# The low parts of the MLP's weights made by VectorE, and a table of places for every early step of an attention and ELU-MLP kernel

## The chip, the cores and the metric

The kernel runs on one core of one Trainium2 chip. The time is the device time of one execution, in microseconds (us). The median of three runs of the kernel before is 1268.88 us (1268.69 to 1268.94). The engines are TensorE (PE in the profile; PEld is its weight load), VectorE (DVE), ScalarE (ACT), GpSimd (POOL) and SyncE (SP), which here issues all transfers.

## The reference

```python
# q, k, v: (8, 12, 448, 64); w_in: (768, 2048); w_out: (2048, 768), all float32
q_n, k_n = rmsnorm(q, g_q), rmsnorm(k, g_k)
scores = q_n @ k_n.T / sqrt(64)
attn = exp(scores - max(scores)); attn = attn / (sum(attn) + 1e-9)
x = (attn @ v).transpose(0, 2, 1, 3).reshape(8 * 448, 768)
h = x @ w_in
g = where(h > 0, h, exp(min(h, 0)) - 1)
out = g @ w_out
```

## The kernel before

The program goes through 8 batches. A batch has 6 pairs of heads, and the 2 x 448 rows of a pair make 7 tiles of 128 rows: 42 tiles a batch, 336 in all, numbered T. For each tile TensorE writes scores of 128x448 to one of five PSUM banks (`s_mm`, L550), VectorE takes the negated maximum (`s_max`, L557), ScalarE the exponential with its sum (`s_exp`, L571), GpSimd adds 1e-9 to the sum and scales it (`s_z`, L575), and VectorE takes the reciprocal (`s_rec`, L583). In the first batch (`by_pe`) GpSimd then makes a diagonal matrix of the reciprocals (`s_diag`, L587), and TensorE multiplies with it, which normalises and transposes at once (`s_pe`, L595); the matmul is in float32. In later batches ScalarE and VectorE write the normalised tile as a float16 high part and low part (`s_hi` L611, `s_lo` L616), and a transfer transposes it (`s_tr`, L626). `attend` (L643) multiplies with v. Its output is the transpose of x, again as high and low part (L650, L657, L662).

The MLP takes every operand as a high and a low part in float16 and adds three products: high by high, high by low, low by high. For one batch it has 16 groups of 18 matmuls with w_in (L738) and 6 groups of 48 with w_out (L752), 576 in all. After each of the 16, `m1_out` makes the ELU in five steps: exp (ScalarE, L675), subtract 1 and cut at 0 (VectorE, L679), maximum with h (VectorE, L685), high part (ScalarE, L690), low part (VectorE, L693).

The weights are prepared once, beside the first batch's attention: w_in in 16 pieces of 128x768 (`conv_in`), w_out in 24 pieces of 128x512 (`conv_out`). Both begin with `conv`: a load, two steps of ScalarE on the bits (L238, L239), a shift (L244) and a join (L268) by VectorE which give the piece w, column sums by 13 or 9 small matmuls with a matrix of ones (L143), and a scale ws from their maximum (L146, L152). Then w_in's piece has: ScalarE makes ws times the identity (L289), GpSimd the high part (L292), TensorE for each half the float32 product of that diagonal with w less the high part (L299, L300), ScalarE copies the two halves out as the low part (L303). w_out's piece has three steps of GpSimd: the product with ws (L323), the high part from it (L328), the low part by subtraction (L334); the low part is stored to DRAM and loaded again for each batch. The column sums of w_out's first 7 pieces go to two banks of their own, those of the others to `av`, which also holds the output of `attend`.

Every engine does its instructions in the order in which the program issues them. That order is written out: time is counted in half-steps h, two for each tile. `SCHED` holds for every step of a piece, pair or batch the h at which it is issued; for tiles it is one row of offsets from 2T for the first batch and one for the rest. `rate` says how many of the MLP's matmuls have been issued by h, with an entry for every 7 half-steps. `run_tasks` issues what stands at h, `s_mm` one tile a step ahead, `attend` at fixed places.

Of the kernel before, what the change touches and what calls it, by code (L numbers as in the profile page):

```python
# [33 lines left out]
def tile_attention_then_elu_mlp(ctx: ExitStack, tc: tile.TileContext, qk, v, v_scan, gg, w_in, w_out, out):  # L34
# [184 lines left out]
    def conv(src, i, width, acol, bank, parts):  # L219
# [14 lines left out]
        def s_act():  # L234

            nc.scalar.activation(t, raw[:, :, 1].bitcast(F32), AF.Abs, scale=2.0**-112)  # L238
# [34 lines left out]
        steps = [load, s_act, s_shift, s_join, on_pe(s_sums), s_scale]  # L273
# [6 lines left out]
    def conv_in(f):  # L280
        hi, lo = (t[f].rearrange("p c n -> p (c n)") for t in (whi, wli))
        half = [slice(0, 384), slice(384, 768)]
        dgw = None
# [26 lines left out]

    def conv_out(i):
# [10 lines left out]
        def s_mult(w, ws):  # L322
            nc.gpsimd.tensor_scalar(  # L323
                out=w, in0=w, scalar1=ws, scalar2=2.0**UP, op0=ALU.mult, op1=ALU.mult
            )

        def s_high(w, ws):
            nc.gpsimd.tensor_scalar(  # L328
                out=hi, in0=view(w), scalar1=1.0, scalar2=0.0, op0=ALU.mult, op1=ALU.add
            )  # L330

        def s_low(w, ws):

            nc.gpsimd.tensor_tensor(out=low(w), in0=view(w), in1=hi, op=ALU.subtract)  # L334

        def s_store(w, ws):
# [3 lines left out]
            w_out, i, WO_W, most[:, i : i + 1], mb[i % 2] if i < WO_OWN else av,  # L340
            [s_mult, s_high, s_low, s_store],
# [133 lines left out]
    def v_steps(b):  # L475
# [16 lines left out]
        def four():  # L492
# [4 lines left out]
            ibits(vs, p2, -1, ALU.mult, (254 + 7 + UP) * E, ALU.add)  # L497
# [3 lines left out]
    def m_steps(b):  # L501
# [3 lines left out]
        sc, u, am, ui = (  # L505
            small(n, NF if n == "sc" else 1, bufs=3 if n == "u" else 2)
            for n in ("sc", "u", "am", "ui")
        )
        mscale[b] = sc, ui, u
# [7 lines left out]
        def powers():  # L517
            if b == 0:
                ibits(a_in, a_in, POWER, ALU.bitwise_and, 0, ALU.bitwise_or)

        def most_of():
# [144 lines left out]
    def m1_out(b, f, ph):  # L666
# [11 lines left out]

# [5 lines left out]

# [12 lines left out]
        return [one, two, three, four, five]  # L697

    def m2_out(b, d, py):
        u = mscale[b][2]  # L700
        y = ua = None

        def one():
# [3 lines left out]
                out=ua, in0=u, scalar1=a_out[:, d : d + 1], scalar2=2.0**-14, op0=ALU.mult,  # L707
                op1=ALU.mult,
# [10 lines left out]
        return [one, two, three]  # L719

    def mlp(b):
# [7 lines left out]
        for f in range(NF):  # L729
# [3 lines left out]
            ph = t_mo()  # L733
            for c in range(NC_):
# [47 lines left out]
    for T in reversed(range(NCHUNK)):  # L782
        k = 2 if by_pe(T) else 1
        hs = [2 * T + h for h in SCHED["tile"][k]]
        j = T % NJ
        if k < 2:
# [52 lines left out]
    for h in range(H0, LAST):  # L839
        T, odd = divmod(h, 2)  # L840

# [3 lines left out]
        ok = lambda t: 0 <= t < NCHUNK  # L845
# [4 lines left out]
        p, r = divmod(h, HP)  # L850

        if ok(T + 1) and odd == (h >= START):
            mm.append(lambda: s_mm(T + 1))
        if r == 7 and 0 <= p - 1 < NP:
# [160 lines left out]
```

## Time and profile before

| | |
|---|---|
| median of the runs | 1268.88 us |
| span of the profiled execution | 1267.6 us |
| TensorE busy | 1211.2 us, 96% |
| VectorE busy | 862.6 us, 68% |
| ScalarE busy | 822.3 us, 65% |
| GpSimd busy | 545.1 us, 43% |

The page gives the span of the profiled execution, from its first to its last instruction, and no other time of it; the median lies 1.3 us above the span. Times within the trace are counted from the span's start. A busy time is the union of an engine's instructions, which overlap a little, so that the sum of durations can be larger. Lines named L are those of the kernel before.

### The profile page before, as it was taken

The page shows a single profiled execution, that of the slowest core. Times are in us where ns is not written, and L with a number is a line of the kernel's source. Part 1 is how long each engine was busy: PE and PEld are TensorE (multiplying, and loading weights), DVE is VectorE, ACT ScalarE, POOL GpSimd, SP SyncE. Part 2 cuts the span into 40 slices and gives each one's busy share as a digit, 9 for nine tenths or more (in the row PEclk, how much of TensorE's full clock was granted, in tenths as well). Part 3 has the DMA queues.
Part 4 walks back from the last instruction along what each step waited for, and adds up shares of the span by engine and source line. Part 5 has one row for each costly group of instructions (what it writes and reads, how often), then busy time and mean ns, then how long its engine had stood idle before and what let it go on. Part 6 is the DMA issues. An engine that isn't in the chain of part 4 may idle for free.

```text
span 1267.6 us, 21938 instructions
## 1 busy us (share of the span) xinstructions
PE 1211.2 (96%) x7276; PEld 745.2 (59%) x7276; DVE 862.6 (68%) x1975; ACT 822.3 (65%) x1737; POOL 545.1 (43%) x879
## 2 busy tenths in 40 slices
PE   4899798899999999999999999999999999999998
PEld 2556444467556665576556755666557755675576
DVE  7767899977787568855886678756875678642410
ACT  7999878855676567754775567756766567542310
POOL 4755886774444433433444344434344334320000
PEclk9999999999999999999999999999999999999999
DMA  8665489989677986689576986698777957762011
GB/s 278 211 169 167 137 204 207 212 176 233 160 164 150 215 181 156 139 193 219 140 165 160 234 162 142 148 218 193 150 150 184 225 138 160 135 158 72 1 48 63
DMA packets 413392, 209.61 MB, mean 165 GB/s; under 512 B 369504, under 2 KB 389600, under 8 KB 413280
## 3 DMA queue, kind: packets, MB, share of 16 engines
q1 hardware_dynamic: 413280, 208.22, 70.9%
q8 instruction: 57, 0.93, 0.3%
q14 instruction: 55, 0.45, 0.1%
HBM read 93.52 MB, written 14.16 MB: 85 GB/s over the span
## 4 chain that ended last, share of the span: by engine, by line
PE 79%; DMA 1%; DVE 1%; SPq 0%; issue 0%; ACT 0%; ACTq 0%
PE m L752 22%; PE m L738 20%; PE s L752 11%; PE s L738 10%; PE s L550 8%; PE av L643 7%; DMA ptall<-p 1%; DVE w32s L268 0%; DVE gall L693 0%; DVE p L616 0%; PE av L143 0%; DVE e L685 0%; DVE st L557 0%; SPq L626 0%; SPq L448 0%
## 5 line engine op out<-in xcount | busy, mean ns | idle before, releaser
L557 DVE TENSOR_REDUCE st<-s 128x1 f32<-128x448 f32 x336 | 208.0, 619 | 154.4 <-PE s L550 152.8
L575 POOL TENSOR_SCALAR st<-st 128x1 f32<-128x1 f32 x336 | 83.7, 249 | 492.4 <-ACT s L571 454.3
L752 PE MATMUL m<-gall,whos 128*128 128x448 f16 x1024 | 282.2, 353 | 0.0
L752 PEld LDWEIGHTS <-whos 128*128 128x128 f16 x1536 | 221.9, 145 | 75.3 <-issue 2.6
L738 PE MATMUL m<-x,whi 128*128 128x448 f16 x916 | 253.9, 354 | 1.0 <-DVE x L657 0.6
L571 ACT ACTIVATE s<-s,st 128x448 f32<-128x448 f32 x294 | 177.9, 605 | 94.0 <-DVE st L557 91.7
L611 ACT ACTIVATE p<-s,st 128x448 f16<-128x448 f32 x294 | 185.1, 630 | 74.0 <-DMA ptall<-p 50.7
L738 PEld LDWEIGHTS <-whi 128*128 128x128 f16 x1536 | 149.5, 98 | 138.8 <-issue 3.9
L616 DVE SCALAR_TENSOR_TENSOR p<-s,st,p 128x448 f16<-128x448 f32 x294 | 198.9, 676 | 30.8 <-ACT p L611 29.1
L550 PE MATMUL s<-qkt 128*128 128x448 f16 (+1 forms) x768 | 184.1, 357 | 13.7 <-ACT gall L605 4.8
L752 PE MATMUL m<-gall,wls 128*128 128x448 f16 x512 | 181.2, 354 | 0.0
L738 PE MATMUL m<-x,wli 128*128 128x448 f16 x458 | 162.2, 354 | 0.0
L752 PE MATMUL s<-gall,whos 128*128 128x448 f16 x512 | 141.6, 353 | 1.3 <-DVE e L685 0.9
L752 PEld LDWEIGHTS <-wls 128*128 128x128 f16 x768 | 110.7, 144 | 41.4 <-issue 7.0
L738 PE MATMUL s<-x,whi 128*128 128x448 f16 x460 | 126.7, 353 | 0.2 <-DVE e L685 0.2
L738 PEld LDWEIGHTS <-wli 128*128 128x128 f16 x768 | 75.2, 98 | 75.6 <-issue 8.3
L690 ACT ACTIVATE gall<-e,ui 128x448 f16<-128x448 f32 x128 | 85.0, 664 | 38.9 <-DVE e L685 38.8
L550 PEld LDWEIGHTS <-qkt 128*128 128x128 f16 (+1 forms) x768 | 62.6, 100 | 78.5 <-issue 36.0
L693 DVE SCALAR_TENSOR_TENSOR gall<-e,ui,gall 128x448 f16<-128x448 f32 x128 | 90.1, 704 | 8.6 <-ACT gall L690 8.6
L643 PE MATMUL av<-ptall,vt 128*64 128x448 f16 x924 | 94.8, 353 | 0.7 <-DMA ptall<-p 0.7
L752 PE MATMUL s<-gall,wls 128*128 128x448 f16 x256 | 90.6, 354 | 0.0
L403 POOL TENSOR_TENSOR nat<-nat,r 128x896 f32<-128x896 f32 (+1 forms) x48 | 82.4, 1716 | 11.0 <-DVE r L393 8.0
(121 smaller groups left out, 1786.6 us busy)
## 6 DMA issues: line engine op xcount, KB each, us to landing
wls<-wl_d SPq DMA_DIRECT2D x48, 512.0 KB, 4.3
nat<-in_qk SPq DMA_DIRECT2D x48, 448.0 KB, 4.5
raws<-in_w_out SPq DMA_DIRECT2D x24, 512.0 KB, 4.4
qkt<-qkt SPq DMA_DIRECT2D x96, 112.0 KB, 4.0
out<-y SPq DMA_DIRECT2D x48, 224.0 KB, 2.7
vn<-in_v SPq DMA_DIRECT2D x38, 256.0 KB, 3.1
vscan<-in_v_scan SPq DMA_DIRECT2D x36, 224.0 KB, 3.7
whos<-in_w_in SPq DMA_DIRECT2D x10, 768.0 KB, 8.2
```

Of the source, the lines that this page charges most:

```text
L403: nc.gpsimd.tensor_tensor(out=n[:, a:], in0=n[:, a:], in1=r[:, a:], op=ALU.mult)
L550: nc.tensor.matmul(ps[r0 : r0 + n, :S], lhs, qq[:, 1, h * S : h * S + S], start=(t == 0), stop=(t == 2),)
L557: nc.vector.tensor_reduce(out=st[:, 0:1], in_=pss[T][:, :S], axis=AX.X, op=ALU.max, negate=True)
L571: nc.scalar.activation(e, ps, AF.Exp, bias=st[:, 0:1], accum_out=st[:, 1:2])
L575: nc.gpsimd.tensor_scalar(out=st[:, 1:2], in0=st[:, 1:2], scalar1=1e-9, scalar2=2.0 ** (UP - 7) if by_pe(T) else 2.0**-7, op0=ALU.add, op1 ...
L611: nc.scalar.activation(p16[:, :S], pss[T][:, :S], AF.Copy, scale=stats[T][:, 2:3])
L616: nc.vector.scalar_tensor_tensor(out=p16[:, S:], in0=ps[:, :S], scalar=r, in1=p16[:, :S], op0=ALU.mult, op1=ALU.subtract)
L643: nc.tensor.matmul(av[64 * h : 64 * h + 64, :S], vs[:, h], ps[h], start=(k == 0), stop=(k == len(terms) - 1),)
L690: nc.scalar.activation(g[:, 0], e, AF.Copy, scale=ui)
L693: nc.vector.scalar_tensor_tensor(out=g[:, 1], in0=e, scalar=ui, in1=g[:, 0], op0=ALU.mult, op1=ALU.subtract)
L738: nc.tensor.matmul(ph[:, :S], w[:, c, :], x[:, r, :], start=(c == 0 and i == 0), stop=last)
L752: nc.tensor.matmul(py[:, :S], w, g[:, r, :], start=(f == 0 and i == 0), stop=last)
```

## The change

The low part of a piece becomes one instruction of VectorE, `w * ws - high`, for both weights; the products on TensorE, their diagonal and the copies go. GpSimd makes w_out's high part directly as `w * ws`. The factor 2**13 of the former products now lies in the matrix of ones and in the later scales. In the first batch ScalarE makes `relu(1 - exp(h))` in place of VectorE's subtraction, and VectorE then takes the minimum with -h, so the sign of g turns and is turned back with the output's scale. The small step `s_z` is done by VectorE in the first batch. All column sums of w_out go to `av`. The table gets a row of its own for each of the first 96 tiles, for each MLP group of the first batch and for each of the first scores and `attend`, and `rate` an entry for each h. `EARLY`, by which parts of the first groups could be issued ahead, is 0.

```diff
-    nc.vector.memset(ones, 1.0)
+    nc.vector.memset(ones, 2.0**-UP)
...
-        steps = [load, s_act, s_shift, s_join, on_pe(s_sums), s_scale]
+        steps = [load, s_act, s_bits, s_shift, s_join, on_pe(s_sums), s_scale]
...
-        def s_diag(w, ws):
-            nonlocal dgw
-            dgw = pool.tile([128, 128], F32, tag="dgw", name="dgw", bufs=2)
-            nc.scalar.activation(dgw, ident, AF.Copy, scale=ws)
 
         def s_high(w, ws):
             nc.gpsimd.tensor_scalar(
-                out=hi, in0=w, scalar1=ws, scalar2=2.0**UP, op0=ALU.mult, op1=ALU.mult
+                out=hi, in0=w, scalar1=ws, scalar2=0.0, op0=ALU.mult, op1=ALU.add
             )
 
         def s_low(w, ws):
-            for i, c in enumerate(half):
-                pss[i] = mb[i]
-                nc.tensor.matmul(pss[i][:, :384], dgw, w[:, c], start=True, stop=False)
-                nc.tensor.matmul(pss[i][:, :384], neg, hi[:, c], start=False, stop=True)
-
-        def s_out(i):
-            nc.scalar.activation(lo[:, half[i]], pss[i][:, :384], AF.Copy)
+            nc.vector.scalar_tensor_tensor(
+                out=lo, in0=w, scalar=ws, in1=hi, op0=ALU.mult, op1=ALU.subtract
+            )
...
-        def s_mult(w, ws):
-            nc.gpsimd.tensor_scalar(
-                out=w, in0=w, scalar1=ws, scalar2=2.0**UP, op0=ALU.mult, op1=ALU.mult
-            )
-
         def s_high(w, ws):
             nc.gpsimd.tensor_scalar(
-                out=hi, in0=view(w), scalar1=1.0, scalar2=0.0, op0=ALU.mult, op1=ALU.add
+                out=hi, in0=view(w), scalar1=ws, scalar2=0.0, op0=ALU.mult, op1=ALU.add
             )
 
         def s_low(w, ws):
-
-            nc.gpsimd.tensor_tensor(out=low(w), in0=view(w), in1=hi, op=ALU.subtract)
+            nc.vector.scalar_tensor_tensor(
+                out=low(w), in0=view(w), scalar=ws, in1=hi, op0=ALU.mult, op1=ALU.subtract
+            )
...
-            w_out, i, WO_W, most[:, i : i + 1], mb[i % 2] if i < WO_OWN else av,
-            [s_mult, s_high, s_low, s_store],
+            w_out, i, WO_W, most[:, i : i + 1], av,
+            [s_high, s_low, s_store],
...
     def s_z(T):
         st = stats[T]
-        nc.gpsimd.tensor_scalar(
+        (nc.vector if by_pe(T) else nc.gpsimd).tensor_scalar(
...
         def two():
-
+            if b == 0:
+                nc.scalar.activation(e, e, AF.Relu, scale=-1.0, bias=one_c)
+                return
...
         def three():
-
+            if b == 0:
+                nc.vector.scalar_tensor_tensor(
+                    out=e, in0=ph[:, :S], scalar=mscale[b][3][:, f : f + 1], in1=e, op0=ALU.mult,
+                    op1=ALU.min,
+                )
+                return
...
-        k = 2 if by_pe(T) else 1
-        hs = [2 * T + h for h in SCHED["tile"][k]]
+        rows = SCHED["tile"]
+        hs = rows[T] if T < len(rows) - 1 else [2 * T + h for h in rows[-1]]
...
+    for T in range(NCHUNK):
+        n = SCHED["mm"][0]
+        pe_at.setdefault(n[T] if T < len(n) else 2 * T - 1, []).append((s_mm, T))
+    for p in range(NP):
+        n = SCHED["att"][0]
+        pe_at.setdefault(n[p] if p < len(n) else HP * p + HP + 7, []).append((attend, p))
...
     "tile": [
-        [-2.5, -1.5, -1.5, -0.5, 0.5, 1.5, 2.5, 5, 3],
+        [0.5, 1, 2, 2.5, 6, 6, 8],
...
-RATE_FROM = 85
+RATE_FROM = 25
```

What the table does to the order is shown at three places. In the rows, lines of before are those of the kernel before, and lines of after are a few lower.

TensorE, after the column sums of the second piece of w_in (bank `s3`). `dgw` is the diagonal, `m0` and `m1` the banks of the products, `qkt` the transposed q and k. Before, and then now:

```order
L143 MATMUL s3_70<-tiny_85,ones_80 128x64
L299 MATMUL m0_73<-w32s_140,dgw_238 128x384
L300 LDWEIGHTS neg_82
L300 MATMUL m0_73<-whi0_95,neg_82 128x384
L299 MATMUL m1_74<-w32s_140,dgw_238 128x384
L300 LDWEIGHTS neg_82
L300 MATMUL m1_74<-whi0_95,neg_82 128x384
L550 LDWEIGHTS qkt_208
L550 MATMUL s0_67<-qkt_208 128x448
```

```order
L542 MATMUL s1_68<-qkt_218 128x448
L542 LDWEIGHTS qkt_218
L542 MATMUL s0_67<-qkt_218 128x448
L542 LDWEIGHTS qkt_218
L542 MATMUL s0_67<-qkt_218 128x448
L542 LDWEIGHTS qkt_218
L542 MATMUL s2_69<-qkt_218 128x448
```

The products of the first piece stood between the sums and the scores of the first tile; now the scores of the first three tiles (banks `s1`, `s0`, `s2`) follow the sums at once, two matmuls each (the first of `s1` stands just ahead).

VectorE, around the maxima of the first tiles. L557 before and L549 now are `s_max`, L583 and L575 the reciprocal, L289 now is the low part of w_in's piece (`wli0`), L567 the small step `s_z`, L268 the join. Before, and then now:

```order
L268 SCALAR_TENSOR_TENSOR w32s_140<-whos_127,wts_139 128x768
L557 TENSOR_REDUCE st_287<-s0_67 128x1
L181 TENSOR_REDUCE mv_265<-gall_136 128x1
L146 TENSOR_REDUCE a_in_143<-av_72 128x1
L152 TENSOR_SCALAR ws_305<-a_in_143 128x1
L557 TENSOR_REDUCE st_308<-s1_68 128x1
L583 RECIPROCAL st_287<-st_287 128x1
L378 TENSOR_REDUCE ss_317<-qkt_300 128x14
```

```order
L289 SCALAR_TENSOR_TENSOR wli0_111<-w32s_140,ws_215,whi0_95 128x768
L549 TENSOR_REDUCE st_284<-s1_68 128x1
L549 TENSOR_REDUCE st_288<-s0_67 128x1
L268 SCALAR_TENSOR_TENSOR w32s_140<-whos_127,wts_139 128x768
L244 TENSOR_SCALAR wts_139<-wts_139 128x768
L549 TENSOR_REDUCE st_298<-s2_69 128x1
L144 TENSOR_REDUCE a_in_143<-av_72 128x1
L150 TENSOR_SCALAR ws_302<-a_in_143 128x1
L567 TENSOR_SCALAR st_284<-st_284 128x1
L567 TENSOR_SCALAR st_288<-st_288 128x1
L549 TENSOR_REDUCE st_312<-s3_70 128x1
L575 RECIPROCAL st_288<-st_288 128x1
```

The low part of the first piece stands ahead of the first two maxima, and the small steps of tiles stand behind the third maximum, together.

GpSimd, among the first pieces of w_out. L323, L328 and L334 before are product, high part and low part, L309 now is the high part; L587 and L579 are the diagonals of the tiles, L575 the small step. Before, and then now:

```order
L323 TENSOR_SCALAR w32s_140<-w32s_140,ws_1429 128x512
L575 TENSOR_SCALAR st_1420<-st_1420 128x1
L328 TENSOR_SCALAR whos_127<-w32s_140 128x512
L587 TENSOR_SCALAR dgz_1487<-ident_75,st_1420 128x128
L417 TENSOR_TENSOR nat_1109<-nat_1109,gst_141 128x448
L334 TENSOR_TENSOR w32s_140<-w32s_140,whos_127 128x512
L575 TENSOR_SCALAR st_1455<-st_1455 128x1
L323 TENSOR_SCALAR w32s_140<-w32s_140,ws_1484 128x512
L328 TENSOR_SCALAR whos_127<-w32s_140 128x512
L587 TENSOR_SCALAR dgz_1521<-ident_75,st_1455 128x128
```

```order
L579 TENSOR_SCALAR dgz_1385<-ident_75,st_1350 128x128
L410 TENSOR_TENSOR t16_1209<-nat_987,t16_1209 128x7x64
L309 TENSOR_SCALAR whos_127<-w32s_140,ws_1365 128x512
L579 TENSOR_SCALAR dgz_1473<-ident_75,st_1356 128x128
L309 TENSOR_SCALAR whos_127<-w32s_140,ws_1419 128x512
L579 TENSOR_SCALAR dgz_1497<-ident_75,st_1407 128x128
L309 TENSOR_SCALAR whos_127<-w32s_140,ws_1480 128x512
L579 TENSOR_SCALAR dgz_1524<-ident_75,st_1469 128x128
```

Between two diagonals GpSimd had up to three instructions of a piece and the small steps; now one instruction of a piece stands there.

## Rows read from the trace of the kernel before

**Rows 1.** The page: span, then busy time, share and count by engine.

```profile
span 1267.6 us, 21938 instructions
PE 1211.2 (96%) x7276; PEld 745.2 (59%) x7276; DVE 862.6 (68%) x1975; ACT 822.3 (65%) x1737; POOL 545.1 (43%) x879
```

**Rows 2.** Stretches: length; busy us (count) of PE, PEld, DVE, ACT, POOL; clock, DMA, GB/s.

```profile
0.00:24.00 24.00, 6.81 (x52) 4.24 (x53) 16.64 (x39) 17.22 (x23) 9.29 (x12) 1.00 0.83 272
24.00:148.00 124.00, 107.40 (x820) 71.00 (x818) 92.70 (x217) 119.57 (x240) 83.80 (x131) 0.99 0.62 185
148.00:314.00 166.00, 147.73 (x947) 88.27 (x947) 142.62 (x309) 122.50 (x242) 117.39 (x159) 0.98 0.90 199
314.00:1152.00 838.00, 837.29 (x4862) 510.57 (x4862) 582.32 (x1364) 537.94 (x1196) 333.33 (x573) 1.00 0.77 170
1152.00:1268.00 116.00, 111.95 (x602) 71.14 (x598) 28.29 (x49) 25.12 (x40) 1.32 (x5) 0.99 0.13 42
...
148.00:256.00 108.00, 91.81 (x601) 48.65 (x601) 101.41 (x215) 88.31 (x169) 81.69 (x105) 0.97 0.87 197
256.00:314.00 58.00, 55.92 (x346) 39.62 (x346) 41.21 (x95) 34.19 (x74) 35.70 (x55) 1.00 0.96 203
```

**Rows 3.** Timeline of VectorE at 313 us: start, length, line, operation.

```profile
313.19 0.61 DVE L557 TENSOR_REDUCE st<-s 128x1 f32<-128x448 f32 x1
```

**Rows 4.** PE's timeline at 44 us; lines: busy us, mean ns, idle before.

```profile
43.95 0.81 PE L299 MATMUL m<-w32s,dgw 128*128 128x384 f32 x2
...
45.56 0.54 PE L550 MATMUL s<-qkt 128*128 128x448 f16 x2
...
L303 ACT ACTIVATE wli<-m 128x384 f16<-128x384 f32 x32 | 15.4, 490 | 0.4 <-PE m L300 0.4
L289 ACT ACTIVATE dgw<-ident,ws 128x128 f32<-128x128 f32 x16 | 6.3, 396 | 0.0
L323 POOL TENSOR_SCALAR w32s<-w32s,ws 128x512 f32<-128x512 f32 x24 | 20.4, 849 | 7.6 <-DVE ws L152 3.7 <-DVE st L583 3.4
L334 POOL TENSOR_TENSOR w32s<-w32s,whos 128x512 f16<-128x512 f32 x24 | 29.6, 1238 | 1.1
L328 POOL TENSOR_SCALAR whos<-w32s 128x512 f16<-128x512 f32 x24 | 17.4, 727 | 1.4
L575 POOL TENSOR_SCALAR st<-st 128x1 f32<-128x1 f32 x336 | 83.7, 249 | 492.4 <-ACT s L571 454.3 <-ACT ex L571 26.6 <-DMA ptall<-p 6.0
...
L679 DVE TENSOR_SCALAR e<-e 128x448 f32<-128x448 f32 x16 | 8.2, 510 | 0.1
```

**Rows 5.** Single lines: duration ns min/median/max, or busy us and mean ns.

```profile
L268 DVE SCALAR_TENSOR_TENSOR w32s<-raws,wts x30: 671/946/1916, 14.6 to 272.0; 128x512 uint32<-128x512 uint32 x24, 128x768 uint32<-128x768 uint32 x6
L268 DVE SCALAR_TENSOR_TENSOR w32s<-whos,wts x10: 940/959/1820, 21.2 to 114.7; 128x768 uint32<-128x768 uint32 x10
...
L268 DVE SCALAR_TENSOR_TENSOR w32s<-raws,wts 128x512 uint32<-128x512 uint32 x18 | 17.7, 995 | 0.6 <-ACT raws L239 0.4
...
L693 DVE SCALAR_TENSOR_TENSOR gall<-e,ui,gall x128: 658/676/1481, 173.6 to 1212.1; 128x448 f16<-128x448 f32 x128
L685 DVE SCALAR_TENSOR_TENSOR e<-m,sc,e x85: 658/675/685, 169.3 to 1207.3; 128x448 f32<-128x448 f32 x85
...
L152 DVE TENSOR_SCALAR ws<-most 128x1 int32<-128x1 int32 x24 | 3.7, 154 | 0.8
...
L690 ACT ACTIVATE gall<-e,ui 128x448 f16<-128x448 f32 x128 | 85.0, 664 | 38.9 <-DVE e L685 38.8
```

**Rows 6.** Timelines of VectorE and GpSimd at 191 us.

```profile
191.66 1.34 DVE L679 TENSOR_SCALAR e<-e 128x448 f32<-128x448 f32 x1
...
191.43 1.32 POOL L334 TENSOR_TENSOR w32s<-w32s,whos 128x512 f16<-128x512 f32 x1
```

**Rows 7.** Lines of ScalarE, 148 to 314 us; PE's waits there: total, times, longest.

```profile
L611 ACT ACTIVATE p<-s,st 128x448 f16<-128x448 f32 x41 | 25.8, 630 | 21.0 <-DMA ptall<-p 12.2 <-DVE st L583 4.2 <-issue 3.4
...
PE av L143 <- DVE x L662: 3.7, 2, 2.4
```

More of the change, by code (lines that the diff above doesn't have):

```diff
@@ L70, in t_mo @@
         taken += 1
-        return mb[taken % 3]
+        return mb[(taken - 1) % 3]
     ident = const.tile([128, 128], F32, name="ident")
@@ L88, in tile_attention_then_elu_mlp @@
     nc.vector.memset(eps, 1e-6)
+    one_c = const.tile([128, 1], F32, name="one")
+    nc.vector.memset(one_c, 1.0)
     def cols(t, n):
@@ L254, in s_scale @@
             e = largest(bank, acol)
-            ws = small("ws")
+            ws = small("ws", bufs=4)
             ibits(ws, e, POWER, ALU.bitwise_xor, POWER, ALU.bitwise_and)
@@ L355, in load_v, with read_v @@
     def load_v(p):
-        if p in vn:
-            return
+        if p >= 2 * NPAIR - 1:
+            read_v(p)
+    def read_v(p):
         vn[p] = pool.tile([128, 4, 2, D], F32, tag="vn", name="vn", bufs=1)
@@ L496, in four @@
             vs = vscale[b] = small("vs")
-            ibits(vs, p2, -1, ALU.mult, (254 + 7 + UP) * E, ALU.add)
+            ibits(vs, p2, -1, ALU.mult, (254 + 7) * E, ALU.add)
         return [one, two, on_pe(three), four]
     def m_steps(b):
[L505 to L509, printed above, removed]
+        sc = u = am = ui = ns = None
         def mul(out, x, s1, s2=None):
@@ L517, in powers, with scales @@
         def powers():
+            nonlocal sc, u, am, ui, ns
+            sc, u, am, ui = (
+                small(n, NF if n == "sc" else 1, bufs=3 if n == "u" else 2)
+                for n in ("sc", "u", "am", "ui")
+            )
+            ns = small("ns", NF) if b == 0 else None
+            mscale[b] = sc, ui, u, ns
             if b == 0:
                 ibits(a_in, a_in, POWER, ALU.bitwise_and, 0, ALU.bitwise_or)
+        def scales():
+            mul(sc, a_in, vpow[b], 2.0 ** (-28 + UP))
+            if b == 0:
+                mul(ns, a_in, vpow[b], -(2.0 ** (-28 + UP)))
         def most_of():
@@ L695, in five @@
             )
-        return [one, two, three, four, five]
+        return SCHED["m1"][f if b == 0 else NF], [one, two, three, four, five]
     def m2_out(b, d, py):
-        u = mscale[b][2]
+        u, sign = mscale[b][2], -1.0 if b == 0 else 1.0
         y = ua = None
@@ L717, in three @@
             nc.sync.dma_start(out=out[d * 128 : (d + 1) * 128, b * S : (b + 1) * S], in_=y)
-        return [one, two, three]
+        return SCHED["m2"][d if b == 0 else NC_], [one, two, three]
     def mlp(b):
@@ L727, in wl_load @@
             nc.sync.dma_start(out=wls[d], in_=wl_d[d])
-        for f in range(NF):
+        early = EARLY if b == 0 else 0
+        runs = [(f, [c]) for c in range(NC_ - 1) for f in range(early)]
+        runs += [(f, [NC_ - 1] if f < early else range(NC_)) for f in range(NF)]
+        phs = {}
+        for f, chunks in runs:
             if f in (8, 12):
@@ L732, in mlp @@
             wh, wl = whi[f], wli[f]
-            ph = t_mo()
-            for c in range(NC_):
+            if f not in phs:
+                phs[f] = t_mo()
+            ph = phs[f]
+            for c in chunks:
                 x = xs[(b * NPAIR + c) % NX]
@@ L849, in tile_attention_then_elu_mlp @@
         mm = []
[L850 to L854, printed above, removed]
-            mm = [lambda mm=mm: (*(fn() for fn in mm), attend(p - 1))]
+        if h in pe_at:
+            mm = [lambda fns=pe_at[h]: [fn(x) for fn, x in fns]]
         parts = len(mm) + 1
@@ L869, in tile_attention_then_elu_mlp @@
         if r:
-            steps_at(h + 1, enumerate(r))
+            put([h + x for x in r[0]], [(fn,) for fn in r[1]])
         if done % 7 == 0:
@@ L963 @@
+        [189.5, 190, 190, 191, 192, 193.5, 195],
+        [189.5, 189.5, 193.5, 193.5, 194, 194.5, 199],
         [0, 1, 2, 3, 4, 4.5, 6, 9, 5],
[1 row of a table removed]
     ],
     "rate": [
-        [6, 10, 50, 98, 150, 190, 248, 296, 342, 394, 444, 493, 549, 576],
[8 rows of a table added]
+    ],
+    "m1": [
+        [1, 3, 3.5, 5.5, 5.5],
+        [1.5, 2, 4.5, 5, 6],
+        [1, 4.5, 5.5, 6.5, 7.5],
+        [1, 2.5, 3.5, 5, 8.5],
+        [1, 2, 3.5, 5.5, 7],
+        [1, 2, 2, 4, 5.5],
+        [2.5, 3.5, 5, 7.5, 10.5],
+        [1.5, 2, 3, 4.5, 5.5],
+        [1, 3, 5, 6, 7],
+        [0.5, 2, 4, 7.5, 9],
+        [0.5, 2, 3, 4, 8.5],
+        [1, 1.5, 4, 7.5, 8.5],
+        [1, 2.5, 2.5, 5.5, 6],
+        [2, 2, 3, 6, 7],
+        [2.5, 3, 6, 6, 7],
+        [1, 3, 4.5, 4.5, 5],
+        [1, 2, 3, 4, 5],
+    ],
@@ L968 @@
+    "m2": [
+        [6.5, 8.5, 9],
+        [8.5, 11, 17.5],
+        [0.5, 10, 15],
+        [7.5, 10, 13.5],
+        [3, 5, 13.5],
+        [2.5, 5.5, 12.5],
+        [1, 2, 3],
+    ],
[6 rows of a table added]
+    ],
+    "att": [
+        [20, 33, 51, 62, 76, 90, 104, 118, 131, 148, 162, 174],
     ],
 }
-WO_OWN = 7
+EARLY = 0
 CK = S // 4
-DIAG_DVE = False
-RATE_FROM = 85
+RATE_FROM = 25
 UP = 13
```

162 lines of the change are left out of this document (122 added, 40 removed), and 124 rows, old and new, of the table SCHED.

## The prediction

> **What bounds the kernel now.** I read the page's totals first, then cut the span into five stretches, then looked at who waits and at single lines inside the stretches that are not full.
>
> The page shows TensorE (PE) busy for 1211.2 of 1267.6 us [rows 1]; only some 56 us of the span are idle on it. The stretches show where these lie [rows 2]. From 314 us on, PE works 837.29 of 838 us, and in the last stretch 111.95 of 116 us, which are only about 112 us long before the last result is written out. Neither has anything to give: the change leaves the batches after the first with the same matmuls. Before 24 us PE works 6.81 us; that is loading and the first chain of normalisation, and it waits for data. What is left is the part from 24 to 314 us: 290 us with 107.40 + 147.73 = 255.1 us of PE work and 34.9 us of idle PE. At 313.19 us the 85th tile's maximum begins [rows 3], the first of the third batch; from there PE is saturated. So the time is 1267.6 us less what these 290 us lose.
>
> Inside them the bound changes. From 24 to 148 us ScalarE works 119.57 of 124 us (0.964), VectorE 92.70. From 148 to 256 us VectorE works 101.41 of 108 us (0.94). From 256 to 314 us PE works 55.92 of 58 us (0.964), while the DMA engines are at 0.96 [rows 2]. So a full engine is packed to 0.94 to 0.96 here, and the others wait on it.
>
> **The change, part by part.** All sums are for the 290 us.
>
> *PE loses the products for w_in's low parts.* One matrix takes from 43.95 us to the next instruction at 45.56 us, 1.61 us [rows 4]. Of 16, two lie before 24 us, where PE waits anyway: 14 x 1.61 = 22.5 us, 255.1 - 22.5 = 232.6 us. This alone gives nothing where ScalarE or VectorE is the bound.
>
> *ScalarE* loses 32 evictions (15.4 us) and 16 scaled identities (6.3 us) [rows 4]. 14 of 16 matrices: 19.0 us less, all in the stretch where it is the bound. It gains 16 relu steps on 128x448; their price is not shown, the nearest row is L690's 664 ns on the same size [rows 5], 10.6 us, taken as an upper bound; at nothing at all the sum would be 10.6 us less. ScalarE: 119.6 + 122.5 - 19.0 + 10.6 = 233.7 us. The order has one table load as before, so I add none for relu.
>
> *GpSimd* loses the 24 multiplications (20.4 us) and the 24 subtractions (29.6 us), and 42 of the small steps at 249 ns (10.5 us); the high part reads the product's input with a scale and costs between L328's 727 ns and L323's 849 ns [rows 4], up to 2.9 us more. 83.8 + 117.4 - 57.6 = 143.6 us of 290.
>
> *VectorE* gains most. (a) 40 low parts, an operation on two tensors in SBUF. For 768 columns the nearest is L268 on 768: 0.94 us at best, 0.96 at the median, 1.82 at worst. For 512 columns L268 took 0.67 us at best and 0.995 us on average between 148 and 314 us, 1.48 times as much [rows 5]. With that factor the 768 go up to 1.39 us. I take the middle of both: 1.1 and 0.85 us. That is 17.6 + 20.4 = 38.0 us, with ends at 31.1 and 46.2. (b) 42 small steps at 154 ns as L152 [rows 5]: 6.3 us. (c) The 16 first-batch subtractions go: L679 took 8.2 us there [rows 4]. (d) VectorE waits less for GpSimd. L268's 18 instructions take 18 x (0.995 - 0.671) = 5.8 us more than at best, L679's 16 x (0.510 - 0.371) = 2.2 us more: 8.0 us. GpSimd keeps 143.6 of 201.2 us of work; I take half the 8.0 back, 4 us, ends 0 and 8. The sum: 235.3 + 38.0 + 6.3 - 8.2 - 4.0 = 267.4 us, ends 256.5 and 279.6.
>
> Why GpSimd enters (d): L679 started at 191.66 us, lasted 1.34 us, against 0.371 at best, and ended with GpSimd's L334 of 191.43 us, 1.32 us [rows 6]. L693, with two SBUF inputs, runs from 658 to 1481 ns; L685, of the same size but with one input in PSUM, never leaves 658 to 685 [rows 5].
> The Trainium skill (SBUF — State Buffer, section "SBUF: two separate sides") says that VectorE and GpSimd share a port pair which whoever starts first holds for a whole instruction, and that a VectorE operation with two SBUF inputs needs it against a GpSimd one that reads SBUF. Rows 5 and 6 agree with it. It speaks against this change: all 40 low parts are such operations, so each could wait for a whole GpSimd instruction; it speaks for it as 48 GpSimd instructions go. What it would make of the time at its worst is the third rival's sum.
>
> *New waits.* In VectorE's queue the low part stands behind GpSimd's high part. Behind `wli0` the maxima of the first two tiles are queued, and ScalarE's exponentials wait for those; the same holds for every matrix. In return the small step after the exponential no longer goes to GpSimd and back, and the diagonal follows it directly. On PE the scores of three tiles stand in a row before the next column sums instead of one, so that less is queued behind each wait. The 7 column sums for w_out that had banks of their own go to the bank of the attention output; PE waited 3.7 us there for L662 [rows 7]. I price these at nothing in sum; if the cover fails it shows as worse packing, and one point of VectorE's packing is 2.9 us.
>
> *Order.* The transfers that stand before the second batch's first transposed tile are the same in kind and count within two, so DMA keeps its 0.62 x 124 + 0.90 x 166 = 226 us.
>
> **The sum.** VectorE with 267.4 us is now the largest of the 290, ahead of ScalarE (233.7) and PE (232.6). Nothing shows how well it will be packed; I take 0.964, which is what the bound engine had in two of the three pieces. 267.4 / 0.964 = 277.4 us, 12.6 us less than 290. The profiled span becomes 1267.6 - 12.6 = 1255.0 us. The page has no other time of its execution than the span; the median of the runs is 1.3 us over it, for what lies around. That gives 1256 us, 1% less. With no change to speak of in the packing of the whole (235.3 of 290 us before) there would be a loss; the forecast rests on VectorE having room from 24 to 148 us, where ScalarE's load falls by 19 us.
>
> **Rivals.**
> 1. *PE's work comes off whole.* VectorE's ends meet the low side (256.5 / 0.964 = 266.1 us) and PE keeps its idle 34.9 us: 232.6 + 34.9 = 267.5 us, 22.5 less, 1246 us. For it: ScalarE and GpSimd both get room, and the hops fall. Against: it needs the low parts near their best price.
> 2. *No gain, as the second batch's start is bound elsewhere.* From 148 to 314 us L611 waited 12.2 us for the transposes to free its buffer [rows 7], DMA was at 0.90 [rows 2], and none of that goes. If these 166 us stay, only the first 124 can shrink: VectorE there has 92.7 + 15.4 (14 low parts) + 6.3 + 4.3 (5 low parts of w_out) = 118.7, at 0.964 123.1 us. Gain 0.9 us: 1268 us. Against: VectorE was the bound from 148 to 256 us, not DMA.
> 3. *Slower: the port.* In 24 to 256 us each low part falls together with a GpSimd instruction, nothing is given back under (d), and VectorE has 279.6 us; with the packing of 0.94 it had when it was the bound, 297.4 us, 7.4 more: 1276 us. It decides from 279.6 us on at 0.964, that is when a low part costs on average (279.6 - 267.4) / 40 = 0.31 us more than the 0.95 taken. For it: L268's average, the queue behind each low part. Against: GpSimd has 58 us less to do.
>
> **How the numbers follow.** Forecast 0.50, first rival 0.20, second 0.13, third 0.17. The forecast's own range is 1250 (packing 0.985) to 1266 us (0.93). Within 0.2%, 2.5 us, is what a measurement of this kernel can't tell from no change. Faster: the first rival, nearly all of the forecast and a little of the second, 0.71; same 0.11; slower 0.18. The range for 8 in 10 goes from 1243, a little beyond the first rival, to 1272 us, between the second and the third.
>
> **What would show it.** Between 24 us and PE's saturation VectorE should be the fullest engine, at 0.95 or more, ScalarE well under its 0.964, GpSimd near one half. The 85th maximum should begin near 300 us, and what follows should be as long as now. The 768-column low part should take 0.95 to 1.4 us, the 512-column one 0.67 to 1.0; at twice their best price the third rival holds. If the first batch's tiles end sooner but the 85th maximum doesn't, it is the second. The forecast is wrong if VectorE has idle time of over 20 us in the stretch, or if PE's stretch after it grows.

## The result and the profile after

The changed kernel takes 1251.23 us (1248.98 to 1251.78), the kernel before 1268.91 us beside it: ratio 0.9852, 95% interval 0.9838 to 0.9866, 17.7 us less. 1256 us was forecast, with 1243 to 1272 as the range. Two readings carry the explanation: where TensorE (PE) stands idle, and what VectorE does up to 300 us.

The page of the changed kernel, span and busy time by engine:

```profile
span 1249.5 us, 21706 instructions
...
PE 1190.1 (95%) x7180; PEld 736.2 (59%) x7180; DVE 867.6 (69%) x2042; ACT 809.9 (65%) x1705; POOL 498.0 (40%) x789
```

Span is PE's busy time plus its idle time. Against [rows 1] PE works 21.1 us less and stands idle 1249.5 - 1190.1 = 59.4 us in place of 56.4. So the 18.1 us of span are 21.1 us of PE's work that went, less 3.0 us of idle time that came. VectorE works only 5.0 us more, GpSimd 47.1 us less.

Its stretches, columns as in [rows 2], then three of its 16 us pieces:

```profile
24.00:148.00 124.00, 94.74 (x786) 64.47 (x786) 110.74 (x304) 115.64 (x219) 79.33 (x93) 0.96 0.69 202
148.00:300.00 152.00, 145.90 (x930) 90.85 (x929) 131.73 (x302) 119.21 (x241) 75.11 (x112) 0.98 0.91 208
300.00:1152.00 852.00, 850.46 (x4926) 516.30 (x4927) 586.15 (x1361) 537.95 (x1194) 333.13 (x568) 1.00 0.78 167
...
24.00:40.00 16.00, 11.11 (x82) 8.74 (x82) 15.50 (x43) 14.23 (x26) 12.49 (x14) 0.79 0.89 294
...
136.00:152.00 16.00, 11.05 (x71) 5.37 (x70) 14.35 (x43) 14.54 (x29) 7.43 (x12) 0.89 0.76 160
...
184.00:200.00 16.00, 15.98 (x120) 8.92 (x119) 15.71 (x40) 15.97 (x34) 7.66 (x12) 1.00 0.84 217
```

The 3.0 us are mainly a balance of two larger changes. From 24 to 148 us PE's idle time grew from 16.6 us [rows 2] to 29.3 us; from there on it fell, from 18.3 us (of 166) to 6.1 us (of 152).

From 24 to 148 us as a whole no engine is full: ScalarE has 115.64 of 124 us (0.93), VectorE 110.74 (0.89). In single pieces one is, such as VectorE with 15.50 of 16 us from 24 us on. From 148 to 300 us PE is the fullest engine (145.90 of 152 us), well before the point at which the prediction let it saturate. The granted clock, 0.99 before in the first stretch, is 0.96. Such a figure is a mean over TensorE's two levels, 1.2 and 2.4 GHz; in the piece in which PE worked 11.11 of 16 us it is 0.79.

VectorE's timelines (start, length) at the first tile of the second batch and, as [rows 3], of the third; first the kernel before, then the changed one:

```profile
147.43 0.60 DVE L557 TENSOR_REDUCE st<-s 128x1 f32<-128x448 f32 x1
```

```profile
134.52 0.61 DVE L549 TENSOR_REDUCE st<-s 128x1 f32<-128x448 f32 x1
...
288.71 0.61 DVE L549 TENSOR_REDUCE st<-s 128x1 f32<-128x448 f32 x1
```

12.9 us are gained by the second batch, 24.5 by the third, and 18.3 remain at the 127th maximum (448.8 and 430.5 us). The 6 us that go again are 4.0 us of work that PE now does behind the 85th maximum and no longer ahead of it, and 2.2 us more idle time there.

VectorE's groups, 24 to 314 us before and 24 to 300 us now (busy us, mean ns, idle before). Before:

```profile
L268 DVE SCALAR_TENSOR_TENSOR w32s<-raws,wts 128x512 uint32<-128x512 uint32 x24 | 24.9, 1045 | 0.6 <-ACT raws L239 0.4
L244 DVE TENSOR_SCALAR wts<-wts 128x512 uint32<-128x512 uint32 x24 | 16.1, 676 | 0.1
...
L583 DVE RECIPROCAL st<-st 128x1 f32<-128x1 f32 x83 | 12.9, 155 | 20.1 <-POOL st L575 19.6
...
L389 DVE SCALAR_TENSOR_TENSOR ss<-ss,r 128x14 f32<-128x14 f32 x24 | 9.1, 380 | 0.4
```

After:

```profile
L314 DVE SCALAR_TENSOR_TENSOR w32s<-w32s,ws,whos 128x512 f16<-128x512 f32 x24 | 20.5, 853 | 0.2 <-POOL whos L309 0.2
L268 DVE SCALAR_TENSOR_TENSOR w32s<-raws,wts 128x512 uint32<-128x512 uint32 x24 | 17.5, 736 | 0.2 <-ACT raws L239 0.2
L289 DVE SCALAR_TENSOR_TENSOR wli<-w32s,ws,whi 128x768 f16<-128x768 f32 x15 | 15.9, 1058 | 0.0
...
L575 DVE RECIPROCAL st<-st 128x1 f32<-128x1 f32 x86 | 12.9, 155 | 3.1 <-POOL st L567 2.6
...
L244 DVE TENSOR_SCALAR wts<-wts 128x512 uint32<-128x512 uint32 x24 | 10.3, 435 | 0.0
...
L567 DVE TENSOR_SCALAR st<-st 128x1 f32<-128x1 f32 x42 | 5.8, 144 | 1.5 <-ACT ex L563 1.3
...
L373 DVE SCALAR_TENSOR_TENSOR ss<-ss,r 128x14 f32<-128x14 f32 x26 | 4.7, 181 | 0.4
```

The new work is there (L314, L289 and L567, 42.2 us), and 17.6 us have gone from three groups that the change doesn't touch: join 7.4 us, shift 5.8, and 4.4 of a Newton step, which refines the inverse roots of the norms on 128x14 (L389, now L373). The reciprocal's wait for GpSimd falls from 20.1 to 3.1 us. Single low parts, in the whole span (ns min/median/max), and the relu:

```profile
L289 DVE SCALAR_TENSOR_TENSOR wli<-w32s,ws,whi x16: 998/1010/1656, 20.3 to 114.2; 128x768 f16<-128x768 f32 x16
L314 DVE SCALAR_TENSOR_TENSOR w32s<-w32s,ws,whos x24: 731/743/1627, 116.5 to 270.1; 128x512 f16<-128x512 f32 x24
L671 ACT ACTIVATE e<-e,one x16: 628/664/696, 152.5 to 228.7; 128x448 f32<-128x448 f32 x16
```

### The profile page after: what moved, and what is told of

The parts are those of the page before. It is cut to its first block, busy times and chain, and to the rows that moved or that the text cites. A ratio compares the mean times of both kernels' runs of the same rounds, so it can differ in the third digit from the quotient of the medians.

```text
span 1249.5 us, 21706 instructions
## 1 busy us (share of the span) xinstructions
PE 1190.1 (95%) x7180; PEld 736.2 (59%) x7180; DVE 867.6 (69%) x2042; ACT 809.9 (65%) x1705; POOL 498.0 (40%) x789
## 4 chain that ended last, share of the span: by engine, by line
PE 76%; DMA 1%; DVE 1%; ACT 1%; issue 0%; SPq 0%; ACTq 0%
PE m L757 22%; PE m L743 19%; PE s L757 11%; PE s L743 10%; PE s L542 8%; PE av L635 7%; DMA ptall<-p 1%; DVE w32s L314 0%; DVE p L608 0%; SPq L618 0%; DVE st L549 0%; ACT p L603 0%; ACT qkt L358 0%; ACT s L563 0%; DVE mv L179 0%
## 5 line engine op out<-in xcount | busy, mean ns | idle before, releaser
L549 DVE TENSOR_REDUCE st<-s 128x1 f32<-128x448 f32 x336 | 207.1, 618 | 150.6 <-PE s L542 148.2
L567 POOL TENSOR_SCALAR st<-st 128x1 f32<-128x1 f32 x294 | 76.5, 260 | 493.6 <-ACT s L563 483.4
L743 PE MATMUL m<-x,whi 128*128 128x448 f16 x926 | 256.5, 353 | 0.9 <-DVE e L679 0.8
L689 ACT ACTIVATE gall<-e,ui 128x448 f16<-128x448 f32 x128 | 84.8, 665 | 34.8 <-DVE e L684 34.8
L635 PE MATMUL av<-ptall,vt 128*64 128x448 f16 x924 | 98.9, 361 | 4.5 <-DVE most L144 2.9
```

Source lines behind the costliest of these rows:

```text
L549: nc.vector.tensor_reduce(out=st[:, 0:1], in_=pss[T][:, :S], axis=AX.X, op=ALU.max, negate=True)
L567: (nc.vector if by_pe(T) else nc.gpsimd).tensor_scalar(out=st[:, 1:2], in0=st[:, 1:2], scalar1=1e-9, scalar2=2.0 ** (UP - 7) if by_pe(T) e ...
L635: nc.tensor.matmul(av[64 * h : 64 * h + 64, :S], vs[:, h], ps[h], start=(k == 0), stop=(k == len(terms) - 1),)
L689: nc.scalar.activation(g[:, 0], e, AF.Copy, scale=ui)
L743: nc.tensor.matmul(ph[:, :S], w[:, c, :], x[:, r, :], start=(c == 0 and i == 0), stop=last)
```

## The experiments

All are edits of the changed kernel; ratios are to the kernel before, from runs on the same chip. In the accounts, PE's idle time is span less busy time on the page.

**1. The edits in the old order** (`old_order`): tiles, pieces, scans and rate at the places of the kernel before.

```diff
-    "tile": [[0.5, 1, 2, 2.5, 6, 6, 8], [0.5, 0.5, 2, 3, 4, 5, 5.5], ...
+    "tile": [[0, 1, 2, 2.5, 3.5, 4.5, 6.5], [2, 3, 4, 4.5, 5.5, 6.5, 8.5], ...
-    "att": [[20, 33, 51, 62, 76, 90, 104, 118, 131, 148, 162, 174]],
+    "att": [[]],
```

> All edits of the change (low parts by VectorE, high parts straight from the product, relu, the small step on VectorE), but in the order of the kernel before: its offsets for tiles, weights, scores, attention and MLP groups. Theory A, the edits bring the gain because they take work from ScalarE, GpSimd and TensorE in the first 150 us and free VectorE from waiting for GpSimd: at least half of the 17.7 us stays, 1251 to 1260 us. Theory B, the gain is the order's: with the old order VectorE's low parts stand in the way of the maxima and nothing is left, 1265 to 1275 us.

1269.53 us, 1.000 (0.9991 to 1.0009). Theory A falls: with all the load taken off, nothing is gained. Stretch 24 to 148 us, the page's line of busy times, then waits from 24 to 148 us (us, times, longest):

```profile
24.00:148.00 124.00, 92.91 (x704) 64.04 (x703) 104.31 (x272) 104.87 (x193) 72.29 (x81) 0.90 0.63 183
...
PE 1196.9 (94%) x7180; PEld 738.9 (58%) x7180; DVE 876.8 (69%) x2042; ACT 814.1 (64%) x1705; POOL 499.4 (39%) x789
...
PEld s L587 <- POOL dgz L579: 21.6, 15, 2.7
POOL dgz L579 <- DVE st L575: 21.1, 15, 3.4
PE s L587 <- POOL dgz L579: 15.1, 12, 2.2
```

ScalarE, 119.57 us in [rows 2], has 104.87 and no engine is full. VectorE now has low parts ahead of the reciprocals; GpSimd's diagonal waits for the reciprocal and PE for the diagonal. PE works 1196.9 us of a span of 1267.9: 14.3 us less than before, and 71.0 us idle, 14.6 more. Of its products' 27.8 us, its other matmuls take half back, which last longer while the granted clock is 0.90, and its waits the rest. The sums are not quite those of the changed kernel: VectorE works 9.2 us more, ScalarE 4.2 us.

**2. Later in the old order** (`late_pe`): the normalising matmul and its copy half a tile later in the first 42 tiles; the diff is against `old_order`.

```diff
-    "tile": [[0, 1, 2, 2.5, 3.5, 4.5, 6.5], ...
+    "tile": [[0, 1, 2, 2.5, 3.5, 5.5, 7.5], ...
```

> All edits in the order of before, where TensorE waited 15.1 us for the diagonals between 24 and 148 us; the normalising product and its copy of the first 42 tiles each stand one half-step later, one line of the table. Theory L, the edits' gain is lost because the reciprocals come later behind the low parts and TensorE stands at the diagonals: the wait for them falls below 8 us and the time to 1258 to 1266 us. Rival, it is the load of VectorE or ScalarE: the wait moves to the copies or to the scores' banks, 1267 to 1272 us.

1278.2 us, 1.0073 (1.0058 to 1.0088), slower than the rival said. PE's wait for the diagonals falls from 15.1 to 1.4 us, and these come in its place:

```profile
PE s L542 <- ACT ptall L597: 12.6, 7, 2.4
ACT ex L563 <- PE s L587: 11.9, 4, 5.9
...
PE s L542 <- ACT gall L597: 9.0, 4, 3.0
```

The scores' banks come free later. Moving these two steps alike for all tiles only moves the wait.

**3. Half of the new table** (`tiles_new`): tiles, scores and `attend` at the new places, all else at the old.

```diff
-    "wi": [[-17, -14, -12, -13.5, -8, -10, -9.5, -5, -2], ...
+    "wi": [[-17, -9.5, -9.5, -8, -7, -8, -6, -5, -3], ...
-    "wo": [[43.5, 60, 63, 65, 66.5, 65, 67, 67.5, 70.5, 74.5], ...
+    "wo": [[59, 63, 63, 64, 65, 66, 68.5, 69.5, 71.5, 72.5], ...
```

> All edits and, of the new order, only the places of tiles, scores and attention; the weights, v, q and k, the MLP's groups and its rate stand as in the kernel before (the last one or two half-steps of one attention output moved behind it). If the gain of the order lies in scores that run further ahead of the normalising products on TensorE, so that these no longer wait for GpSimd's diagonals, most of it shows: 1252 to 1260 us. If it lies in the places of the weights' steps between the tiles' steps, 1263 to 1272 us.

1324.83 us, 1.0426 (1.0403 to 1.0449), far beyond both theories. The stretch shows every engine waiting, at a granted clock of 0.83:

```profile
24.00:148.00 124.00, 84.67 (x607) 60.00 (x606) 87.11 (x230) 89.30 (x163) 59.04 (x68) 0.83 0.52 156
```

So these places alone gain nothing. The other half, the rest at the new places and the tiles at the old, was not run, and which part of the table makes the gain stays open.

**4. The old division of work in the new order** (`old_ops`, `wi_pe`, and with other buffers and places `old_ops2`, `wi_pe2`). `wi_pe` and `wi_pe2` put w_in's low parts back to PE and ScalarE; the other two put w_out's parts, the small step and the subtraction back too. In all four some of w_in's low parts are mixed with a neighbouring piece's; the work is the same. The MLP's first 8 matmuls come later in all four. The copies of the low parts stand 1 and 1.5 half-steps behind their products in `old_ops` and `wi_pe`, 2.5 and 3.5 in `old_ops2` and `wi_pe2`.

```diff
-            w_in, f, WI_W, a_in[:, f : f + 1], sb[4 - f] if f < 2 else av, [s_high, s_low],
+            w_in, f, WI_W, a_in[:, f : f + 1], sb[4 - f] if f < 2 else av,
+            [s_diag, s_high, on_pe(s_low), lambda w, ws: s_out(0), lambda w, ws: s_out(1)],
```

> The new order with the old operations: w_in's low parts by TensorE and ScalarE, w_out's product, high and low part by GpSimd, the ELU's subtraction by VectorE, the small step by GpSimd. The MLP's first 8 matmuls come later (from half-step 73 on), as the products use their banks. Theory A: most of the gain goes, 1261 to 1270 us. Theory B: most of it stays, 1250 to 1258 us.

> The changed kernel with w_in's low parts alone undone: diagonal by ScalarE, products by TensorE, two copies by ScalarE. TensorE gets 25.8 us, ScalarE 16 to 22 us more, VectorE 16 us less (the profile of the changed kernel shows 1095 ns for one low part of 768 columns). ScalarE worked 115.6 of the 124 us from 24 to 148 us; if it is the bound there, as theory A has it, the 43rd maximum comes 8 to 14 us later and the time is 1257 to 1266 us. If VectorE is the bound, it is 1247 to 1253 us.

> The new table with all four old divisions of the work (w_in's low parts by TensorE and ScalarE, w_out's three steps by GpSimd, the small step by GpSimd, the subtraction by VectorE); against the first run of this kind the diagonals have three buffers and the copies of the low parts stand 2.5 to 3.5 half-steps later. Theory J (the edits only pay in the order made for them, and the order only with the edits): slower than before, 1275 to 1300 us, the 43rd maximum after 155 us. Rival O (the order is what gains, and the first run was slow by its buffers and places): 1255 to 1268 us, the 43rd maximum before 147 us.

> The changed kernel, w_in's low parts alone by TensorE and ScalarE as before, with three buffers for the diagonals and the copies 2.5 to 3.5 half-steps later than in the first try. Theory S (ScalarE's load decides): ScalarE gets 19 us more, 115.6 + 19 = 135 us at 0.96 make 140 in place of 124 us: 1262 to 1270 us, ScalarE over 0.95 from 24 to 148 us. Rival H (the first try was slow by what stood behind the copies): ScalarE's waits for the products fall from 12 us to under 4 us and the time is 1253 to 1261 us.

`old_ops` 1299.25 us, 1.0234 (1.0216 to 1.0251); `old_ops2` 1300.63, 1.0251 (1.0233 to 1.0269); `wi_pe` 1279.75, 1.0076 (1.0061 to 1.0091); `wi_pe2` 1281.56, 1.0095 (1.0075 to 1.0114). `old_ops` and `wi_pe` are slower than either of their theories; `old_ops2` is at the upper end of theory J. So the order, with the old work at these places in it, doesn't gain, and more buffers and later copies don't help. But of `wi_pe2` neither theory holds: ScalarE has only 100.76 of 124 us, and it waits 11.5 us for the products. The stretch 24 to 148 us, then ScalarE's and PE's waits there:

```profile
24.00:148.00 124.00, 100.34 (x702) 65.75 (x701) 69.27 (x204) 100.76 (x204) 54.55 (x69) 0.90 0.52 154
...
ACT wli L308 <- PE m L305: 11.5, 4, 6.6
```

```profile
PE s L560 <- ACT ptall L615: 6.0, 6, 2.2
PE m L304 <- ACT dgw L299: 4.6, 2, 2.3
```

The copies stand in ScalarE's queue ahead of exponentials while PE is behind. Their places are mine, and others might wait less: what w_in's part is worth by itself stays open, and so does what the new order would give the old work at its best places.

**5. w_out's parts back to GpSimd** (`wo_pool`).

```diff
-            nc.vector.scalar_tensor_tensor(
-                out=low(w), in0=view(w), scalar=ws, in1=hi, op0=ALU.mult, op1=ALU.subtract
-            )
+            nc.gpsimd.tensor_tensor(out=low(w), in0=view(w), in1=hi, op=ALU.subtract)
...
+            [s_mult, s_high, s_low, s_store],
```

> The changed kernel with w_out's parts alone undone: product, high and low part by GpSimd. GpSimd gets 50 us more, VectorE loses 24 low parts (18.6 us). Theory P, VectorE's operations on two SBUF tensors wait for GpSimd's: the joins, shifts and Newton steps get back about 20 us, VectorE's busy time stays within 5 us and the time is 1250 to 1258 us. Rival: no such wait, VectorE's busy time falls by 15 us or more and the time by 0 to 4 us, to 1247 to 1251 us.

1261.06 us, 0.9937 (0.9923 to 0.9952), 9.8 us over the changed kernel. VectorE loses 24 low parts (20.5 us) and works only 7.9 us less on the page (859.7): the rest got longer, by less than theory P had it, and the time lies beyond both theories. Two of its groups, 24 to 314 us (the join took 736 ns in the changed kernel, and the reciprocal waited 3.1 us):

```profile
L268 DVE SCALAR_TENSOR_TENSOR w32s<-raws,wts 128x512 uint32<-128x512 uint32 x24 | 19.8, 831 | 0.6 <-DMA wl_d<-w32s 0.6
...
L578 DVE RECIPROCAL st<-st 128x1 f32<-128x1 f32 x87 | 13.1, 155 | 16.0 <-POOL st L570 15.5
```

**6. GpSimd loaded** (`high_thrice`): it makes each high part of w_out three times, 48 instructions and 36.8 us more.

```diff
-            nc.gpsimd.tensor_scalar(
+            for _ in range(3):
+                nc.gpsimd.tensor_scalar(
```

> The changed kernel, but GpSimd makes each of w_out's 24 high parts three times, the same values to the same place: 48 more GpSimd instructions of about 0.7 us, 34 us, and nothing else moved. Theory P, VectorE's operations on two SBUF tensors wait for GpSimd's: its joins, shifts and Newton steps lengthen, VectorE's busy time grows by 8 to 20 us over the 867.6 us of the changed kernel and the time by 3 to 12 us, to 1254 to 1263 us. Rival: GpSimd has room (79 of 124 and 75 of 152 us busy), VectorE's busy time stays within 3 us and the time at 1250 to 1253 us, apart from what the later high parts hold up.

1274.3 us, 1.0031 (1.0016 to 1.0046): 23 us more than the changed kernel, beyond both theories. VectorE's own lengthening is what P said, 10.0 us (877.6 on the page), as in the first row (435 ns in the changed kernel); the rest shows as waits, which leave PE idle for 17.1 us more: the low part's for its high part and PE's for the diagonals (8.5 us, 9 times, in the changed kernel):

```profile
L244 DVE TENSOR_SCALAR wts<-wts 128x512 uint32<-128x512 uint32 x24 | 14.9, 625 | 0.0
...
L315 DVE SCALAR_TENSOR_TENSOR w32s<-w32s,ws,whos 128x512 f16<-128x512 f32 x24 | 21.8, 907 | 7.2 <-POOL whos L310 7.2
...
PE s L588 <- POOL dgz L580: 16.9, 13, 4.3
```

**7. The small step, and the subtraction, back alone** (`sz_pool`, `elu_dve`).

```diff
-        (nc.vector if by_pe(T) else nc.gpsimd).tensor_scalar(
+        nc.gpsimd.tensor_scalar(
```

```diff
-            if b == 0:
-                nc.scalar.activation(e, e, AF.Relu, scale=-1.0, bias=one_c)
-                return
...
```

> The changed kernel with the small step back on GpSimd. GpSimd gets 42 x 0.25 = 10.5 us, VectorE loses 42 x 0.144 = 6.0 us. Theory Q (queues: the step goes to GpSimd and back ahead of the reciprocal): 1254 to 1262 us, VectorE's waits for st from GpSimd over 5 us from 24 to 148 us. Rival E (VectorE's sum decides): 6 us less work of it, 1245 to 1251 us.

> The changed kernel with the first batch's subtraction back on VectorE. VectorE gets 16 x 0.37 to 0.51 = 6 to 8 us, ScalarE loses 16 x 0.644 = 10.3 us, nearly all of it behind 148 us. Theory W (from there TensorE is the bound): 1249 to 1254 us. Rival V (VectorE's load decides, as the prediction had it): 8 us at a packing of 0.96 more: 1257 to 1260 us.

`sz_pool` 1255.78 us, 0.9897 (0.9873 to 0.9921); `elu_dve` 1255.47, 0.9889 (0.9872 to 0.9907). The first is theory Q's low end, with its waits (VectorE's, then PE's):

```profile
DVE st L575 <- POOL st L567: 9.9, 9, 2.3
```

```profile
PE s L587 <- POOL dgz L579: 15.4, 16, 2.4
```

VectorE worked 3.1 us less on the page than in the changed kernel, and the kernel was 4.5 us slower: here the sum doesn't decide. The second lies between its two theories. Its first batch ends as early (133.5 us), and then it takes 58.6 us from the 57th to the 71st maximum, 5.1 more than the changed kernel; why is not shown.

**8. Column sums apart from `attend`** (`sums_m1`): the sums of w_in's pieces from the third on and of w_out's first 7 go to a bank of the MLP.

```diff
-            w_in, f, WI_W, a_in[:, f : f + 1], sb[4 - f] if f < 2 else av, [s_high, s_low],
+            w_in, f, WI_W, a_in[:, f : f + 1], sb[4 - f] if f < 2 else mb[1], [s_high, s_low],
-            w_out, i, WO_W, most[:, i : i + 1], av,
+            w_out, i, WO_W, most[:, i : i + 1], mb[1] if i < WO_OWN else av,
```

> The changed kernel, with the column sums of w_in's pieces from the third on and of w_out's first 7 pieces in bank m1, which the MLP uses only later, in place of the bank of the attention output. TensorE waited there 3.8 us at 64 us, 2.2 us at 78 us and some 2 us more for VectorE's reads of that bank before 148 us. If these waits are on the path, 1244 to 1249 us; if ScalarE (115.6 of 124 us busy) or VectorE sets the pace, 1249 to 1252 us.

**1246.01 us, 0.9809 (0.9793 to 0.9825): faster than both kernels**, and where the first expectation put it. Its page:

```profile
span 1245.6 us, 21707 instructions
...
PE 1190.2 (96%) x7180; PEld 738.0 (59%) x7180; DVE 868.6 (70%) x2042; ACT 810.0 (65%) x1705; POOL 499.3 (40%) x789
```

The same work on every engine within 1.3 us, and PE idle 55.4 us, 4.0 less. In the changed kernel PE's matmuls of `attend` and of the sums waited for each other's results to be read from the bank `av` that they share, 4.3 us for w_in's `a_in` (longest 3.8) among them, from 24 to 148 us:

```profile
PE av L635 <- DVE a_in L144: 4.3, 2, 3.8
PE av L141 <- DVE x L649: 2.2, 1, 2.2
```

Before, the second stood there as well, and the first did not:

```profile
PE av L143 <- DVE x L657: 2.1, 1, 2.1
```

So the wait that came is that of `attend` for a sum of w_in, which lay in this bank before too: it comes with the new places and not with the 7 sums of w_out, for which the prediction named the bank [rows 7]. The run moves both sets of sums and doesn't part them.

## Why the prediction was right, and where it wasn't

*Direction and place: right.* The gain is made before 300 us, 12.9 us of it by the second batch, and kept; behind 300 us PE is as full as before (850.46 of 852 us).

*Prices of the new work: right.* The low parts took 17.5 us for w_in, with the one before 24 us, and 20.5 us for w_out: 38.0 us, as taken. 42 small steps 5.8 us, 6.3 taken. The relu's 664 ns is the bound taken. PE's products were 27.8 us of busy time against 16 x 1.61 = 25.8, of which 14, 22.5 us, were counted.

*Mis-sized: term (d), VectorE's relief from GpSimd.* 4 us were taken, 8 the end. With 34.8 us of low parts, 3.1 of small steps and 5.6 less for the subtraction (busy time by line, overlaps taken out) VectorE should have 32.3 us more; it has 5.0. So 27 us came off lines that were not edited; by the same account it is 21 us in `old_order`, so most of this belongs to the edits and not to the order. The term was worked out from two lines, the join and the subtraction. The shift with one SBUF input (676 to 435 ns) and Newton steps of 128x14 (380 to 181 ns) were left out. `wo_pool` and `high_thrice` confirm the cause from the other side: as GpSimd's work is put back or added, the join (736 to 831 ns) and the shift (435 to 625 ns) get longer, and the 27 us become 17 and 19 us.

*The step that failed: VectorE as the bound of the stretch, packed to 0.964.* VectorE worked 110.74 + 131.73 = 242.5 of 276 us, 0.88, and stood idle 33.5 us; the prediction named over 20 us of it as what would refute it. It is still the largest sum, but barely: PE has 94.74 + 145.90 = 240.6 us. That the forecast's time came out was luck: a sum too large by some 25 us met a packing taken too high, and the measured sum at 0.964 would have forecast some 26 us less. The first stretch as a whole is bound by no one engine; what remains are the waits of the queues on each other: `old_order` has nearly the same sums and no gain. Which part of the new order shortens these waits no run shows by itself. The first rival's frame was closer, PE's work off and its idle time kept: 21.1 us less work, 3.0 us more idle, where it had 22.5 and 0. The products gave 27.8 us, but `attend` took 4.7 us and the scores 2.1 us longer by busy time, with the same matmuls, in part at the lower granted clock (0.96 for 0.99 from 24 to 148 us).

*New waits at nothing in sum: right for this table only.* PE's wait for diagonals from 24 to 148 us grew from 3.2 to 8.5 us, since GpSimd waits for the reciprocals, which stand in VectorE's queue. Before, and then now:

```profile
PE s L595 <- POOL dgz L587: 3.2, 6, 0.9
POOL dgz L587 <- DVE st L583: 6.7, 12, 1.2
```

```profile
PE s L587 <- POOL dgz L579: 8.5, 9, 1.8
POOL dgz L579 <- DVE st L575: 18.0, 12, 5.0
```

Sums and `attend` in one bank cost some 5 us (`sums_m1`), and the reciprocal's wait lost 17.0 us. In the old order the waits cost what the longer matmuls left of PE's freed work.

*GpSimd* fell by 47.1 us, not 57.6: its remaining instructions got longer, such as its 128x896 product from 1728 to 1776 ns. That fits VectorE's low parts holding it up in turn: up to the third batch the product went from 1831 to 1974 ns, behind that it stayed (1689 and 1691).

*Rivals.* The second (no gain, DMA) fell: the 85th maximum came 24.5 us sooner, with DMA at 0.91 from 148 us on (0.90 before). The third (the port) fell in size: a low part cost 0.95 us on average, where 1.26 was its point. Single ones met it: 1.656 and 1.627 us against 0.998 and 0.731 at best. The Trainium skill (SBUF — State Buffer, section "SBUF: two separate sides") also names VectorE's two-port modes beside two SBUF inputs as what needs the shared pair. That fits the shift's stretching (676 ns before, 435 now), and [rows 6] as well, where L679 has one SBUF input; the prediction used only the second half of the sentence. And `high_thrice`, at 1.0031, shows that this rival's direction is real once GpSimd has 37 us more to do.

## What to carry to other kernels

Where engines work in the order of issue, sums of busy time say what may be gained, not what will be: taking 21.7 us of copies and identities [rows 4] off the fullest engine gave nothing in the old order. Account a result as busy plus idle time of the engine that is full later, and look for shared banks among its last waits. When work leaves GpSimd, price every VectorE line that shares SBUF with it by its best time, small ones too.

## What was not expected of the hardware

Steps of VectorE on only 14 columns took 380 ns on average beside a GpSimd that worked 201.2 of 290 us, 1020 ns at worst, and 181 ns beside one that worked 154.4 of 276 us. GpSimd's 36.8 us of added work made VectorE's 10.0 us longer and the kernel 23 us. And the granted clock from 24 to 148 us differed much between these kernels: 0.99 with TensorE busy for 107.40 of 124 us before [rows 2], 0.90 with 92.91 in the old order and 0.83 with 84.67 in `tiles_new`. It doesn't follow the busy time alone: `wi_pe2` had 0.90 with 100.34, the changed kernel 0.96 with 94.74.
